# The attention output computed with tokens on partitions, turned back by a DMA transpose from the fifth pair of chunks on, and the order of operations planned anew

## The chip, the cores and the metric

The kernel runs on one core of a Trainium2 chip. The metric is the device time of one execution in microseconds. Three runs of the kernel before gave 177.81 us as the median (177.77 to 180.62). The profile is of one execution, taken by the hardware profiler.

The engines are named as in the profile: PE is TensorE (matmuls; PEld is its weight loads), DVE is VectorE, ACT is ScalarE, POOL is GpSimd and SP is SyncE, which here only issues DMAs. L756 is line 756 of the kernel before; lines of the changed kernel lie 33 to 91 further down.

## The reference

A gated linear attention (4 batches x 8 heads, 768 tokens, head size 48) is followed by a feed-forward layer with a squared ReLU (3,072 tokens, 384 to 2,048 to 384). Inputs and output are float32.

```python
for t in range(S):                       # q, k, v, alpha: (4, 8, 768, 48)
    state = alpha[:, :, t, :, None] * state + np.einsum('bhd,bhe->bhde', k[:, :, t], v[:, :, t])
    y[:, :, t] = np.einsum('bhd,bhde->bhe', q[:, :, t], state)
x = y.transpose(0, 2, 1, 3).reshape(B * S, H * D)        # (3072, 384)
h = x @ w_in                                             # w_in (384, 2048)
r = np.maximum(h, 0.0)
out = (r * r) @ w_out                                    # w_out (2048, 384)
```

## The kernel before

**Tiling.** The 3,072 tokens are 24 chunks of 128, worked as 12 pairs (g = 0 to 11). Three pairs are one batch. In a pair, tokens 2p and 2p+1 lie on partition p, so that a tile holds 256 tokens, and each chunk c of the pair is one half of the partitions. All 8 heads go together.

**Stages of a pair.** Four loads bring alpha, k, q and v (384 KB each as counted by the profile, line 474, SP queue) into one of four RAW buffers. *decay* takes logarithms, sums them over the tokens on PE (L502, L504), takes exponentials on ACT and scales q and k on DVE (qks, L523). *turned* transposes qks, so that features lie on partitions (qkt): on PE in the first three pairs, from the fourth on by a DMA transpose of 16 blocks of 128x128 on the SP queue (L586). *scores* (L634) multiplies q and k in quarters of the array (64x64), and DVE applies the causal mask (pm, L644). *carry* (L663) adds the pair to the state (DVE L681, POOL L683). *mixed* (L702) computes y: 48 matmuls of masked scores with v (pm, vbf) and up to 24 of q with the state before the chunk (qkt, sbf). In the first pair of a batch the first chunk has no state, and 12 of the 24 fall away. v and the state are the stationary operand and 128 columns move, so y comes out with features on partitions, as the next stage needs it. As a head has 48 features and a matmul gives 64 rows, heads are cut into 12 shares. ACT copies y from PSUM to XT (L739).

**Feed-forward layer.** *up*: 8 units of 6 matmuls a pair (L756, 128x256), ACT ReLU (L760), DVE square (L762, gt). *down*: 8 units of 4 matmuls a pair (L780, 128x384), after every fourth an ACT copy (L787) and a store of 192 KB on the SP queue (L789). The last chunk's down is cut in two halves (L800).

**Weights.** w_in and w_out come in four pieces each on the POOL queue (L446, L449), cast to bf16 on the way; the first waits for alpha of pair 1. The loads of pair 2 wait for the second piece of w_out (OPENS).

**What sets the order.** Nothing is ordered by hand. Each stage adds operations with a work in ns and a due time `at`, counted in half pairs: `2 * g + OFF[name]` (EARLY for pairs 0 and 1, MID for pair 2). A list scheduler (`order`) goes through a model of the engines and of the DMA queues and puts, on each engine, the due operation that is ready first in its queue. It fixes the order of instructions on each engine and each DMA queue; on the chip each engine goes through its list in order and waits on semaphores. The model has constants: LATENCY between engines, RESERVE added to every hand-over after the start, LATE added to the landing of loads, rates of transfers (PAIR, ROWS, TURN), SWITCH for the change between full and quartered array on PE. Where PE is planned to be idle before the first down, `fill` puts matmuls on zeros (L769, `busy`), 512 columns each.

Of the kernel before, what the change touches and what calls it, by code (L numbers as in the profile page):

```python
# [15 lines left out]
class Op:  # L16


    def __init__(self, n, eng, fn, work, at, dma=None, nbytes=0, rate=0.0):
# [7 lines left out]
        self.form = None  # L27


class Program:  # L30
# [4 lines left out]
    RESERVE, LATE = 200, 1200.0  # L35
    AHEAD = 4
    BEGIN = {"SP": 1200.0, "POOL": 2200.0}
    LANDING = {"SP": 900.0, "POOL": 1400.0}
    PAIR, ROWS, TURN = 320.0, 390.0, 135.0
    PACKET = {PAIR: 384.0, TURN: 256.0}  # L40
    LONG = 1792.0
    HOLD = 2500.0
    SWITCH, STICK = 95.0, 1.0

# [7 lines left out]
    def add(self, eng, fn, work, at, reads=(), writes=(), dma=None, nbytes=0, rate=0.0, behind=None, form=None,  # L52
            drain=None):
# [25 lines left out]
        op.form = form  # L79
# [3 lines left out]
    def order(self):  # L83
# [26 lines left out]
        def transfer(limit):  # L110

            while now[0] < limit:
# [20 lines left out]
                if queue[first][0][1] <= 1e-3:  # L133
                    op = queue[first].pop(0)[2]
                    op.landed = op.landed0 = end + self.LANDING[first]
                    if op.at > -2 and op.rate == self.PAIR:
                        op.landed += self.LATE
                    if first == "SP":
                        landed.append(op.landed0)
# [10 lines left out]
        form = None  # L150
        while left:
# [38 lines left out]
            if e == "PE":  # L190
                if op.form != form:
                    op.work += self.SWITCH
                form = op.form
            free[e] = t + op.work
# [21 lines left out]
        self.programs = programs  # L216

# [85 lines left out]
def bass_gla_recurrent__then__act_relu_squared_kernel(  # L303
# [31 lines left out]
    NS, NU, NAC, NRO = 5, 3, 3, 2  # L335
    NGT, NRR, NOS = 3, 4, 8
# [17 lines left out]
    XT = sb("xt", [128, KT, G * TW], BF16)  # L354
# [72 lines left out]
    WH = 4  # L427
    FIRST = 2
    TURN = 3
    SELF = 12  # L430


    RUNS = [(1, 3, 8)]
    OPENS = {2: 5}
    pieces = [(w, n) for w in ("in", "out") for n in range(WH)]
    last_weight, last_load = [None], [None]

    def weights(at, run):
        x0 = sum(r[2] for r in RUNS[:run])
        w0, j0, n0 = RUNS[run]  # L440
        for x in range(x0, x0 + n0):
            which, i = pieces[x]
            gate = raw(w0, j0) if x == x0 else []
            if which == "in":
                w = DFF // WH
                fn = lambda g, i=i, w=w: g.dma_start(WIN[:, :, i * w:(i + 1) * w], win_src[:, :, i * w:(i + 1) * w])  # L446
            else:
                w = FT // WH
                fn = lambda g, i=i, w=w: g.dma_start(WOUT[:, i * w:(i + 1) * w, :], wout_src[:, i * w:(i + 1) * w, :])  # L449
            last_weight[0] = add("POOL", fn, 770, at, reads=gate, writes=[("w" + which, i)], dma=f"w{which}{i}",  # L450
                                 nbytes=DM * DFF * 4 // WH, rate=(305.0, 305.0, 370.0, 370.0, 395.0)[min(x, 4)],
# [12 lines left out]
    def loads(g, at):  # L464
        b, t0, r = g // NW, (g % NW) * TW, g % NRAW
        for j, src in ((3, alpha), (0, k), (1, q), (2, v)):
            s = src[b, :, t0:t0 + TW, :].rearrange("h (p i) d -> p h (i d)", i=2)
            dst = RAW[:, r, j, :].rearrange("p (h e) -> p h e", h=H)
            gate = [("w" + pieces[OPENS[g]][0], pieces[OPENS[g]][1])] if g in OPENS and j == 3 else []
            cuts = (0, 1) if g == 0 and j == 3 else (None,)  # L470
            for X in cuts:
# [5 lines left out]
                                   nbytes=TW * HD * 4 // len(cuts), rate=pr.PAIR, behind=last_load[0])  # L477
# [9 lines left out]
    def decay(g, at):  # L487
# [19 lines left out]
        add("PE", sums, 265, at + 0.02, reads=lab + ["hinc"], writes=[key])  # L507
# [388 lines left out]
```

## Time and profile before

| | |
|---|---|
| median of three runs | 177.81 us (177.77 to 180.62) |
| the profiled execution | 177.77 us, its span 175.8 us |
| granted TensorE clock | 1.000 |
| PE / DVE / ACT / POOL busy | 168.7 / 116.5 / 116.2 / 18.6 us |
| up matmuls L756 | 576, 74.3 us busy |
| down matmuls L780 | 368, 71.2 us busy |
| y matmuls L702 | 576 and 240, 10.4 and 8.6 us busy |
| first up unit, last PE matmul starts | 17.1 us, 173.1 us |
| traffic | 31.83 MB, 75,993 packets |

Busy times of PE overlap: a matmul's length in the profile covers its way through the array, and the next one starts before it ends. What a group of matmuls takes is read from start to start in the timeline. Idle time of an engine that is not on the chain that ended last costs nothing. "issue" is time in which the engine waited for nothing that the profile shows.

### The profile page before, as it was taken

How to read it: one execution, taken by the hardware profiler on the slowest of the kernel's cores; microseconds unless marked ns; L12 is line 12 of the kernel's file. 1: busy time of each engine (PE TensorE's matmuls, PEld its weight loads, DVE VectorE, ACT ScalarE, POOL GpSimd, SP SyncE). 2: the span in 40 equal slices, each digit the busy share in tenths (PEclk: the TensorE clock that was granted, in tenths of full speed). 3: DMA queues.
4: the chain of work that ended last, by engine and by line, in shares of the span. 5: the costliest groups of instructions: out<-in, count | busy, mean ns of one | idle time of the engine just before them, and what ended most of it. 6: DMA issues, size and time to landing. Idle time of an engine off the chain costs nothing.

```text
span 175.8 us, 6062 instructions
## 1 busy us (share of the span) xinstructions
PE 168.7 (96%) x2648; PEld 123.7 (70%) x2648; DVE 116.5 (66%) x251; ACT 116.2 (66%) x235; POOL 18.6 (11%) x35
## 2 busy tenths in 40 slices
PE   7889979999999999999999999999999999999994
PEld 2556658775677777777777776777777777767763
DVE  7895925589979597887965966946836733621410
ACT  4774555695885888879788869747546544645631
POOL 4089300001100201001002001001002000000000
PEclk9999999999999999999999999999999999999999
DMA  5999999999999999999999998901901701101112
GB/s 131 303 300 179 197 203 244 278 318 301 239 248 277 250 261 246 307 180 306 243 235 312 258 265 239 141 28 50 164 4 48 164 4 48 45 4 45 45 45 90
DMA packets 75993, 31.83 MB, mean 181 GB/s; under 512 B 69184, under 2 KB 75968, under 8 KB 75968
## 3 DMA queue, kind: packets, MB, share of 16 engines
q1 hardware_dynamic: 72256, 28.32, 65.0%
q0 software_dynamic: 3712, 3.15, 11.6%
q8 instruction: 20, 0.33, 0.7%
q14 instruction: 5, 0.04, 0.1%
HBM read 25.17 MB, written 4.72 MB: 170 GB/s over the span
## 4 chain that ended last, share of the span: by engine, by line
PE 87%; DVE 3%; ACT 3%; DMA 3%; issue 2%; SPq 1%
PE psH L756 35%; PE psO L780 34%; PE psG L702 8%; PE psG L634 4%; DMA raw<-in_q_dram 3%; DVE pm L644 2%; PE psG L663 2%; ACT xt L739 2%; PE psO L800 2%; PE psG L502 1%; DVE qks L555 1%; ACT rr L760 1%; SPq L474 1%; PE psG L574 1%; DVE ust L681 1%
## 5 line engine op out<-in xcount | busy, mean ns | idle before, releaser
L760 ACT ACTIVATE rr<-psH 128x512 bf16<-128x512 f32 x96 | 56.9, 599 | 35.5 <-PE psH L756 34.6
L756 PE MATMUL psH<-xt,win 128*128 128x256 bf16 x576 | 74.3, 273 | 0.5 <-ACT xt L739 0.4
L780 PE MATMUL psO<-wout,gt 128*128 128x384 bf16 x368 | 71.2, 326 | 0.0
L756 PEld LDWEIGHTS psH<-xt,win 128*128 128x128 bf16 x576 | 54.8, 98 | 13.9 <-ACT xt L739 0.8
L762 DVE TENSOR_TENSOR gt<-rr 128x512 bf16<-128x512 bf16 x96 | 39.8, 425 | 36.7 <-ACT rr L760 36.3
L780 PEld LDWEIGHTS psO<-wout,gt 128*128 128x128 bf16 x368 | 34.5, 98 | 17.2
L644 DVE TENSOR_TENSOR pm<-psG,mask 128x512 bf16<-128x512 f32 x48 | 30.9, 684 | 1.2 <-PE psG L634 1.2
L523 DVE TENSOR_TENSOR qks<-raw,asb 128x768 bf16<-128x768 f32 x20 | 18.4, 956 | 8.1 <-ACT asb L512 8.1
L683 POOL TENSOR_TENSOR sbf<-ust,acp 128x192 bf16<-128x192 f32 x16 | 8.8, 551 | 119.1 <-DVE ust L681 119.1
L739 ACT ACTIVATE xt<-psG 128x384 bf16<-128x384 f32 x24 | 12.6, 596 | 6.6 <-PE psG L702 6.6
L787 ACT ACTIVATE osb<-psO 128x384 f32<-128x384 f32 x23 | 11.4, 494 | 5.2 <-PE psO L780 4.8
L702 PEld LDWEIGHTS psG<-pm,vbf 64*64 64x64 bf16 x576 | 8.4, 107 | 3.7 <-issue 1.8
L702 PE MATMUL psG<-pm,vbf 64*64 64x128 bf16 x576 | 10.4, 218 | 0.6 <-DVE qks L555 0.3
L493 DVE TENSOR_TENSOR raw<-raw 128x384 f32<-128x384 f32 x20 | 10.6, 551 | 0.0
L512 ACT ACTIVATE asb<-psG 128x384 bf16<-128x384 f32 x20 | 9.9, 495 | 1.1 <-PE psG L504 0.8
L702 PE MATMUL psG<-qkt,sbf 64*64 64x128 bf16 x240 | 8.6, 220 | 1.0 <-issue 1.0
L634 PEld LDWEIGHTS psG<-qkt 64*64 64x64 bf16 x384 | 5.8, 106 | 4.3 <-issue 2.4
L634 PE MATMUL psG<-qkt 64*64 64x128 bf16 x384 | 8.1, 219 | 0.6 <-ACT qkt L617 0.4
L769 PE MATMUL psO<-warm 128*128 128x512 bf16 x22 | 7.5, 463 | 1.1 <-DVE warm L391 1.1
L485 ACT ACTIVATE vbf<-raw 128x768 bf16<-128x768 f32 x10 | 8.4, 841 | 0.0
L681 DVE TENSOR_TENSOR ust<-psG,sbf 128x192 f32<-128x192 f32 x15 | 5.3, 355 | 2.6 <-POOL sbf L683 1.9
L498 ACT ACTIVATE lab<-raw 128x384 bf16<-128x384 f32 x10 | 5.2, 520 | 2.2 <-DVE raw L493 2.2
(65 smaller groups left out, 99.5 us busy)
## 6 DMA issues: line engine op xcount, KB each, us to landing
raw<-in_k_dram SPq DMA_DIRECT2D x12, 384.0 KB, 5.0
raw<-in_q_dram SPq DMA_DIRECT2D x12, 384.0 KB, 5.6
raw<-in_v_dram SPq DMA_DIRECT2D x12, 384.0 KB, 5.4
out_dram<-osb SPq DMA_DIRECT2D x23, 192.0 KB, 2.0
raw<-in_alpha_dram SPq DMA_DIRECT2D x11, 384.0 KB, 4.5
win<-in_moe_w_in_dram POOLq DMA_DIRECT2D x4, 384.0 KB, 7.9
wout<-in_moe_w_out_dram POOLq DMA_DIRECT2D x4, 384.0 KB, 12.4
raw<-in_alpha_dram SPq DMA_DIRECT2D x2, 192.0 KB, 2.8
```

The lines of the kernel that those rows point to most:

```text
L493: add("DVE", lambda e: e.tensor_tensor(dst, a0, a1, ALU.mult), 470, at_, reads=reads, writes=writes)
L512: add("ACT", lambda act, z=z: act.activation(ASB[a][:, z, 0, :], ps[:, 0:HD], AF.Exp, scale=2.0 * z - 1.0), 372, at + 0.04 + 0.02 * z, rea ...
L523: add("DVE", lambda dve, z=z, decays=decays: dve.tensor_tensor(QKS[x][:, z, :, :, 0:D], both(r, z), decays, ALU.mult), 870, at + 0.05 + 0. ...
L634: last = pe.matmul(banks[i, j // 2][0][64 * c:64 * c + 64, col:col + 128].rearrange("p (a b) -> p a b", a=2), QKT[t][64 * i:64 * i + 64, 0 ...
L644: add("DVE", lambda dve, i=i, X=X, ps=ps: dve.tensor_tensor(PMB[m][:, i, 2 * X:2 * X + 2].rearrange("p j n s -> p j (n s)"), ps[:].rearran ...
L702: last = pe.matmul(o, lhsT, rhs, start=(c, n % 2) not in begun, stop=True, skip_group_check=True)
L739: add("ACT", lambda act, ps=ps, base=base: act.activation(XT[:, :, base:base + C].rearrange("f k (p i) -> f k i p", i=2), ps[:, 0:HD].rear ...
L756: last = pe.matmul(ps[:, f * TW:(f + 1) * TW], WIN[:, kt, fj * 128:(fj + 1) * 128], XT[:, kt, g * TW:(g + 1) * TW], start=(kt == 0), stop= ...
L760: add("ACT", lambda act: act.activation(RR[r][:], ps[:], AF.Relu), 480, at, reads=[key], writes=[key, ("rr", r)])
L762: add("DVE", lambda dve: dve.tensor_tensor(gt[:, 2 * u:2 * u + 2, :], rr, rr, ALU.mult), 340, at, reads=[("rr", r)], writes=[("gt", g % NG ...
L780: last = pe.matmul(ps[:, 0:DM], GT[g % NGT][:, fj, tt * 128:(tt + 1) * 128], WOUT[:, fj, :], start=(fj == 0), stop=(fj == FT - 1))
L787: add("ACT", lambda act: act.activation(OSB[o][:], ps[:, 0:DM], AF.Copy), 372, at, reads=[key], writes=[key, ("osb", o)])
```

## The change

1. From the fifth pair on (`BACK = 4`), `mixed_back` takes the place of `mixed`. The masked scores and q are stationary and v or the state moves: 64 matmuls with 48 columns and up to 32 more, y with tokens on partitions. ACT copies it to a new tile YB, contiguously, and a DMA transpose of 6 blocks on the SP queue writes XT. Tokens are in another order there, so the store of these pairs writes rows of the output two apart.
2. XT becomes a ring of six pairs (`NX`), [chunk, block, token] within a pair; up reads it with a view of two chunks.
3. In `mixed` the matmuls with the state become operations of their own.
4. w_in comes in five pieces of 2, 2, 4, 4 and 4 blocks; the w_out pieces are issued as a second run that waits for v of pair 1. The loads of pair 2 wait for the first piece of w_out.
5. The warming matmuls in gaps have 128 columns instead of 512. The changed kernel's PE list has 95, the first seven of them with 512 columns as before; the kernel before has 22.
6. The scheduler gets other constants, a model of PE's instruction blocks (`take`), and other due times. Up of pairs 3 to 11 is due at +1.092 instead of -1.226 half pairs.

```diff
-    RESERVE, LATE = 200, 1200.0
+    RESERVE, LATE = 0, 400.0
+    LATE_BACK = 1000.0
...
-    PAIR, ROWS, TURN = 320.0, 390.0, 135.0
-    PACKET = {PAIR: 384.0, TURN: 256.0}
+    PAIR, ROWS, TURN, EARLY = 325.0, 390.0, 135.0, 200.0
+    PACKET = {PAIR: 120.0, TURN: 256.0}
...
+    BLOCK, AHEAD_OF_ALL, FETCH, CALM, BUSY_UNTIL = 256, 37, 5200.0, 1800.0, 36000.0
+    FILL, SHARE = 58.0, 0.75
...
+                filling = filling and n not in until
+                if filling and used > self.AHEAD_OF_ALL:
+                    gap = 2 * int(max(0.0, t - free[e]) * self.SHARE / self.FILL)
+                    used, there = self.take(used, gap, free[e], 100.0, there)[:2]
+                used, there, late = self.take(used, op.size + 1, t, op.work, there)
+                op.work += late
...
+    def take(self, used, size, t, work, there):
+        late = 0.0
+        block = used // self.BLOCK
+        for b in range(block + 1, (used + size) // self.BLOCK + 1):
+            at = t + late + work * (b * self.BLOCK - used) / size
+            late += max(0.0, there.get(b, 0.0) - at)
+            there[b + 1] = max(at, there.get(b, 0.0)) + self.FETCH - (self.CALM if at > self.BUSY_UNTIL else 0.0)
+        return used + size, there, late
...
-    XT = sb("xt", [128, KT, G * TW], BF16)
+    XT = sb("xt", [128, 2 * NX, KT, C], BF16)
+    YB = sb("yb", [128, 2, HD], BF16, NY)
...
-    RUNS = [(1, 3, 8)]
+    RUNS = [(1, 3, 5), (1, 2, 4)]
...
+    CUTS = {"in": (0, 2, 4, 8, 12, 16), "out": (0, 4, 8, 12, 16)}
...
+    def mixed_back(g, at):
+        t, m, vb, b_ = g % NQT, g % NPM, g % NV, g % NY
+        banks = [bank() for c in range(2)]
+        chunks = [1] if g % NW == 0 else [0, 1]
+        def before(pe, swap):
+            for j in range(NP):
+                for i in range(2):
+                    c = i ^ swap
+                    for n in range(2):
+                        if c in chunks:
+                            h = 2 * j + i
+                            last = pe.matmul(banks[c][0][64 * n:64 * n + 64, D * h:D * h + D],
+                                             QKT[t][64 * i:64 * i + 64, 1, n, j, 64 * c:64 * c + 64],
+                                             SBF[(2 * g + c) % NS][64 * i:64 * i + 64, D + PAD * j:2 * D + PAD * j],
+                                             start=False, stop=True, skip_group_check=True)
+            return last
+        def mm(pe):
+            for h in range(H):
+                for i in range(2):
+                    for c in range(2):
+                        for n in range(2):
+                            last = pe.matmul(banks[c][0][64 * n:64 * n + 64, D * h:D * h + D],
+                                             PMB[m][64 * c:64 * c + 64, h % 2, h // 2, i, 64 * n:64 * n + 64],
+                                             VBF[vb][64 * c:64 * c + 64, i, h, 0:D],
+                                             start=(h, i) == (0, 0), stop=True, skip_group_check=True)
+            return last
...
+            add("ACT", lambda act, c=c, ps=ps: act.activation(YB[b_][:, c, :], ps[:, 0:HD], AF.Copy), 400, at + 0.02 * c + 0.01,
+                reads=[key], writes=[key, ("yb", b_, c)])
+        dst, src = XT[:, 2 * (g % NX):2 * (g % NX) + 2].rearrange("f c k t -> f (c k) t"), YB[b_][:].rearrange("p c f -> p (c f)")
+        add("SP", lambda sp: sp.dma_start_transpose(dst, src), 600, at + 0.04, reads=[("yb", b_, c) for c in range(2)],
+            writes=[("xt", g % NX, c) for c in range(2)], dma="back", nbytes=128 * 2 * HD * 2, rate=pr.TURN)
+
+    def store(o, n, cols=slice(None)):
+        rows, tile = out[n * C:(n + 1) * C, cols], OSB[o][:, 0:DM if cols == slice(None) else cols.stop - cols.start]
+        if n // 2 >= BACK:
+            rows = rows.rearrange("(p i) d -> i p d", i=2)
+        return rows, tile
...
-    OFF = dict(decay=-5.14, turned=-4.136, scores0=-2.842, scores1=-2.061, carry=-3.412, mixed=-1.443, up=-1.226)
-    EARLY = dict(decay=-6.102, turned=-5.566, scores0=-5.314, scores1=-4.089, carry=-5.284, mixed=-3.871, up=-2.03)
-    MID = dict(decay=-5.605, turned=-4.806, scores0=-3.382, scores1=-3.16, carry=-4.451, mixed=-1.982, up=-1.395)
+    OFF = dict(decay=-4.416, turned=-4.123, scores0=-1.903, scores1=-1.843, carry=-2.618, mixed=-1.2, up=1.092)
+    EARLY = dict(decay=-6.061, turned=-5.402, scores0=-5.065, scores1=-3.942, carry=-5.21, mixed=-3.405, up=-1.781)
+    MID = dict(decay=-4.77, turned=-4.502, scores0=-4.464, scores1=-4.122, carry=-3.472, mixed=-1.224, up=-0.846)
```

## The prediction

> **What bounds the kernel now.** I read the totals, then the chain that ended last, then TensorE (PE) in order of time, then the transfers. From the page: span, busy time by engine, the DMA row of the 40 slices (4.4 us each, tenths), one DMA queue, and the chain's shares.
>
> ```profile
> span 175.8 us, 6062 instructions
> ...
> PE 168.7 (96%) x2648; PEld 123.7 (70%) x2648; DVE 116.5 (66%) x251; ACT 116.2 (66%) x235; POOL 18.6 (11%) x35
> ...
> DMA  5999999999999999999999998901901701101112
> ...
> q8 instruction: 20, 0.33, 0.7%
> ```
>
> PE is busy for 96% of the span and carries 87% of the chain, so a PE microsecond saved after the start counts in full, and so does one in which PE stands. The DMA row says that transfers are no spare resource either: 16 engines are full until about 114 us. The last row is PE's own instruction stream being fetched: 0.33 MB in 20 packets, about 16 KB each. PE's timeline has the one place where that shows (start, length, engine, line, operation, number):
>
> ```profile
> 21.62 0.22 PE L702 MATMUL psG<-qkt,sbf 64*64 64x128 bf16 x2
> 22.85 0.35 PE L702 MATMUL psG<-qkt,sbf 64*64 64x128 bf16 x10 [1.01 <-issue]
> ```
>
> Twelve matmuls of one group, with no wait among them, are cut in two by 1.01 us of "issue". By the packets' start times a 16 KB packet ran from 20.52 to 21.47 us, and PE went on 1.38 us after its end: it had run out of instructions. A steady pair of chunks reads so:
>
> ```profile
> 116.33 0.82 PE L756 MATMUL psH<-xt,win 128*128 128x256 bf16 x6
> 117.08 0.86 PE L702 MATMUL psG<-pm,vbf 64*64 64x128 bf16 x48
> 117.77 0.34 PE L702 MATMUL psG<-qkt,sbf 64*64 64x128 bf16 x12
> 117.94 0.42 PE L663 MATMUL psG<-vbf,qks 64*64 64x48 bf16 x32
> 118.19 0.37 PE L702 MATMUL psG<-qkt,sbf 64*64 64x128 bf16 x12
> ```
>
> From start to start: 48 matmuls with 128 columns take 0.69 us (14.4 ns each), 32 with 48 columns 0.25 us (7.8 ns). An up unit is 0.655 us, a down unit 0.65; the 0.75 us from 116.33 to 117.08 leaves 0.1 for a change between full and quartered array.
>
> **The change, part by part** (against the profiled execution: 177.77 us, span 175.8 and 2.0 around it; median of the runs 177.81).
>
> 1. *The y matmuls.* Pairs 4 to 11 leave 72 matmuls with 128 columns (72 x 14.4 ns = 1.03 us) for 96 with 48 (96 x 7.8 = 0.75): 0.28 us less, six times. In pairs 6 and 9, first of a sequence, one chunk has no state: 60 x 14.4 = 0.86 against 80 x 7.8 = 0.62: 0.24 less, twice. Sum **-2.2 us**, all on the path.
> 2. *Changes of array shape.* In the built order I count 54 after the first up unit, 50 before: 4 x 0.1 = **+0.4**.
> 3. *Waits that go.* The stall of 1.01 us at 21.84 goes, since the same block boundary now falls about 19 us into the run, in the up units of pair 0: **-1.0**. The only other PE wait above 0.3 us after 26 us is the up units of pair 2 for xt (0.39 at 47.01); in the new order a down unit more stands ahead of them: **-0.4**. What is late next is part 4.
> 4. *The instruction stream.* PE has 5,325 records (2,648 loads, 2,648 matmuls, 29 separate waits) for 20 packets, some 266 each, or blocks of 256 with a little there at the start. With 60 + 2.04 per matmul the cut above lies on 768 = 3 x 256, and the last seven packets begin 1.1 to 1.3 us after PE enters a block: entering one sends for the next, and one only. From the fourth to the fourteenth packet, among full DMA queues, the median is 1.4 us. So a block is there 1.4 + 0.97 + 1.38 = 3.75 us after PE enters the one ahead of it (3.5 where DMA is idle; 5.8 at the stall above). If PE uses up 256 instructions faster, it stands. Before, mixed and carry of a pair are 104 matmuls, 212 instructions, and by this count no two boundaries after 26 us are nearer than 4.9 us. After, they are 128 matmuls, 261 instructions in about 1.1 us. Going down the new order with the durations above, these distances are below 5 us: block 8 to 9 3.5 us, 10 to 11 1.55, 12 to 13 3.15, 15 to 16 3.8, 19 to 20 2.9. The shortest has 4 matmuls of an up unit, then mixed and carry of pair 5, and hardly any MoE work in it. Shortfall against 3.75 (3.5 in the last): 0.25 + 2.2 + 0.6 + 0 + 0.6 = **+3.7**. Bounds: +2.9 if every block takes 3.5 us, +8 if every one takes 4.9 (the slowest of the fourth to fourteenth); nothing at all is a rival. I take the median. The 73 more warming matmuls (95, 88 of them with 128 columns, for 22 with 512) bring the first boundaries earlier; there PE waits 0.3 to 0.6 us at a time for DVE and ACT anyway, which hides some 0.6 us.
>    The Trainium skill ("Runtime: NRT & Kernel Launch", section "Instruction fetch mechanics") also has blocks of 16 KiB with 256 instructions, but says that the next page is fetched while the current one runs and that a crossing is mostly hidden. The trace agrees for 19 crossings and disagrees for the one with 1.01 us. By that rule of the Trainium skill part 4 is nought and the time 174.6 us.
> 5. *The transpose back.* Eight more DMA transposes of 6 blocks of 128x128, where the old ones have 16. An old one alone is 2,048 packets of 256 bytes in 3.1 us (123.80 to 126.88), issue to landing 5.4. The new one is not in the trace: by bytes 6/16 x 3.1 = 1.2 us, if the price is per call 3.1. I take 1.2. It lies between mixed and up of a pair, which the new due times set 2.3 half pairs apart (before 0.2), some 14 us; it is hidden there. On SP it waits for ACT's copy, and the next pair's alpha load and a store stand behind it; who waits for those are the products of a pair needed 20 us later. Cost nothing; without cover, see the second rival. ACT's copies become contiguous (596 ns each before; 494 in L787, same size): 0.1 us off 16 times, off the path.
> 6. *Attention runs ahead.* Up of a pair now comes late, so mixed of pair 7 stands after 49 up and 40 down units where it stood after 56 and 47: 14 units, 9.1 us sooner; the last mixed 17 units, 11 us. Loads and transposes must come so much sooner. DMA per pair: loads 5.4 us (three pairs in 28.66 to 46.17, less two stores), transpose 3.1, two stores 1.4, back 1.2: 11.1 us. PE between the scores of pairs 4 and 11 has 77 us, 11.0 a pair. That just fits, with no reserve where there was one of some 25 us. I cost it at nothing: PE's stalls of part 4 give DMA 3 us.
> 7. *The start.* Weights in nine pieces (first two half as large, one more issue on POOL, 0.8 us), the loads of pair 2 gated by the first piece of w_out, not the second (2.5 us sooner). The first up unit waited for no weights: at 17.14 it follows scores of pair 1, which wait for the raw loads' chain, and that stands. PE is busy 7.49 of the 8.90 us up to 26: at most 1.4 us to win, as much to lose if w_out's last piece comes later. Nothing, +-1.4.
> 8. *Stores in token pairs*: packets of 1,536 bytes as before; the end (2.4 us after the last matmul) stays. Reserve and transfer constants only act through the order.
>
> Sum: -2.2 + 0.4 - 1.0 - 0.4 + 3.7 = +0.5, so **178.3 us**, practically no change.
>
> **The rivals.**
> A. *The blocks come in time.* If the sequencer holds more than one block ahead, or my count is off by some 30 instructions where distances are short, part 4 is nought and the sum is -3.2: **174.6 us**; with the 1.4 us of part 7, 173.2. For it: 19 silent crossings. Against it: none of those was nearer than 4.9 us. The section of the Trainium skill named in part 4 ("Instruction fetch mechanics") would have it this way.
> B. *Slower: scores wait for the DMA queue.* If a transpose back costs as much as a large one (3.1 us), DMA needs 13.0 us a pair against 11.0: over the seven pairs 14 us late, less the 3 us that PE stands anyhow and 5 us by which the earlier loads can be drawn ahead: **184 us**. It decides from about 1.6 us per transpose (7 x 0.5 is then more than the 3 us). For it: DMA is at 9 throughout, and the SP instruction itself took 2 to 3.9 us at the old transposes. Against it: their packets take 18 ns each, and bytes set the time.
> C. *The turned y costs what it saves.* If the 48-column matmuls are limited by weight loads so that each takes 10.5 ns, 96 cost 1.01 us and part 1 is nought: 180.5 us. Against it: carry's 32, with the same shape, run at 7.8.
>
> **How the numbers follow.** Forecast (part 4 between 2.5 and 8 us, 177 to 182.6): 0.50. A: 0.28. B: 0.15. C or something in the start: 0.07. About 2% (3.5 us) is what a measurement of this kernel can tell from no change, as its three runs reach from 177.77 to 180.62. Faster by that is below 174.3: half of A, 0.14. Slower is above 181.4: B and the upper end of the forecast, 0.22. Within: 0.64. The range 173.3 to 183.5 leaves out part of B and a little of A.
>
> **What would show it.** Part 1: in the new trace mixed's 64 plus 32 matmuls take 0.75 us. Part 4: "issue" gaps of 0.3 to 2.5 us inside groups without waits, the largest in mixed of pair 5, each about 1.4 us after a 16 KB packet ends; A has none. Part 6 and B: PE idle ahead of the scores, released by the transpose's DMA, growing from pair to pair. Part 7: the first up unit at 17 us and continuous PE from 26. I am wrong if PE's gaps after 26 us are below 1 us in all, or if they stand at the scores.

## The result, and the profile after

The changed kernel takes **204.54 us** (median of 4 runs, 203.41 to 205.78) against 177.79 us of the kernel before in the same session (177.18 to 180.62): a ratio of 1.152 (95% interval 1.143 to 1.161), 27 us slower. The forecast was 178.3 us, in a range of 173.3 to 183.5. Some executions of one kernel are up to 4% slower than its others; the ratios here and below leave these out, the medians and ranges have them in.

From the page of the changed kernel: span and instructions, busy time by engine, then the 40 slices (5.0 us each) of PE, of its clock, of the DMA engines and of what they moved, and the chain's shares.

```profile
span 201.4 us, 6601 instructions
...
PE 175.9 (87%) x2905; PEld 127.9 (63%) x2905; DVE 119.6 (59%) x251; ACT 114.5 (57%) x235; POOL 20.4 (10%) x36
...
PE   7889899999999995999999859948995999999900
...
PEclk9999999999999998799999997996998899999985
DMA  5999999999999689994989698988877002111111
GB/s 147 282 262 183 202 209 288 298 318 219 320 229 274 160 244 226 173 302 87 319 135 148 182 192 74 252 172 99 80 84 107 27 32 63 46 42 39 36 50 39
...
PE 68%; DMA 12%; SPq 6%; issue 4%; ACT 3%; DVE 2%; DVEq 0%
```

Three things stand in it. PE is busy for 175.9 us, 7 more than before, yet the span is 25.6 longer: PE has holes (the 5s and the 4) and nothing to do in the last two slices. The DMA row ends in 1s that never stop: in the last 35 us 36 to 63 GB/s flow without a pause, where the kernel before had 0s between its bursts. And DMA has gone from 3% of the chain to 12%.

PE's last matmul ends at 191.05 us, 10.3 us ahead of the end of the span; before it was 2.4. All that runs there is the stores. These are two stretches of the changed kernel (from:to, length, five engines' busy time, PE clock, share of the 16 DMA engines, GB/s), after PE's last matmul:

```profile
191.40:196.40 5.00, 0.00 (x0) 0.00 (x0) 0.00 (x0) 0.02 (x1) 0.00 (x0) 0.89 0.13 50
196.40:201.40 5.00, 0.00 (x0) 0.00 (x0) 0.00 (x0) 0.00 (x0) 0.00 (x0) 0.50 0.12 39
```

and this a stretch of 0.8 us of the kernel before with a single store in it:

```profile
158.60:159.40 0.80, 0.80 (x7) 0.49 (x5) 0.00 (x0) 0.13 (x1) 0.00 (x0) 1.00 0.68 246
```

A share of 0.13 is two engines of 16, and it stays at 0.13 while a queue of stores is waiting. By the packets' times a store of 192 KB, 128 packets of 1,536 bytes and about 65 ns each in both kernels, has 2 packets in flight on the mean (12.8 before) and takes 3.9 to 5.3 us where one with nothing beside it took 0.67 (158.65 to 159.32). The last six stores of whole chunks ran one after the other from 167.76 to 196.42 us, and the last two halves after them.

Earlier on it is the loads that pay. PE's waits in the changed kernel (engine, line, what it waited for: us, times, longest):

```profile
PE psH L843 <- ACT rr L849: 5.9, 2, 3.6
PE psH L843 <- issue: 2.2, 1, 2.2
PE psO L870 <- issue: 2.1, 1, 2.1
...
PE psG L667 <- issue: 0.8, 1, 0.8
PE psG L696 <- issue: 0.6, 1, 0.6
```

The first is the largest, and the chain that ended last shows what is behind ACT's relu there (start, length, what):

```profile
109.60 2.25 SPq L507
111.89 7.25 DMA raw<-in_v_dram
119.16 0.84 ACT vbf L518
120.00 0.49 ACT rr L849
120.54 1.46 PE psH L843 x6
```

The load of v, issued on the SP queue, needed 7.25 us to land, ACT's cast of v waited for it, and the relu that PE's next up unit needs stood in ACT's queue behind that cast. The other 3.6 us, at 136.81, have the same chain. What is issued while such stores run is late: by its packets' times the transpose back took 4.5 us at 121.64 and 4.3 us at 137.97, against 1.1 us (69.52 to 70.63) with no store in its way.

The "issue" waits are stops for instructions, part 4 of the prediction. PE's timeline around the largest, in pair 5 (start, length, line, operation, count):

```profile
75.79 1.27 PE L843 MATMUL psH<-xt,win 128*128 128x256 bf16 x10
79.29 0.59 PE L843 MATMUL psH<-xt,win 128*128 128x256 bf16 x2 [2.23 <-issue]
...
80.15 1.44 PE L870 MATMUL psO<-wout,gt 128*128 128x384 bf16 x4
81.38 1.87 PE L843 MATMUL psH<-xt,win 128*128 128x256 bf16 x10
```

A down unit of 4 matmuls takes 1.24 us to the next start here, where a warm one takes 0.65: after the stop PE's clock is down (the 8 and the 7 in PEclk), by the trace's clock records to half for 3.41 us.

### The profile page after: what moved, and what is told of

It is laid out like the page before. It is cut to its first block, busy times and chain, and to the rows that moved or that the text cites. A ratio compares the mean times of both kernels' runs of the same rounds, so it can differ in the third digit from the quotient of the medians.

```text
span 201.4 us, 6601 instructions
## 1 busy us (share of the span) xinstructions
PE 175.9 (87%) x2905; PEld 127.9 (63%) x2905; DVE 119.6 (59%) x251; ACT 114.5 (57%) x235; POOL 20.4 (10%) x36
## 3 DMA queue, kind: packets, MB, share of 16 engines
q0 software_dynamic: 4112, 3.15, 10.3%
## 4 chain that ended last, share of the span: by engine, by line
PE 68%; DMA 12%; SPq 6%; issue 4%; ACT 3%; DVE 2%; DVEq 0%
PE psH L843 28%; PE psO L870 26%; DMA raw<-in_v_dram 7%; SPq L507 4%; PE psG L667 3%; DMA raw<-in_alpha_dram 3%; DMA raw<-in_k_dram 2%; PE psG L803 2%; PE psG L735 2%; DVE qks L588 1%; PE psO L890 1%; PE psG L696 1%; SPq L879 1%; ACT rr L849 1%; PE psO L858 1%
## 5 line engine op out<-in xcount | busy, mean ns | idle before, releaser
L843 PE MATMUL psH<-xt,win 128*128 128x256 bf16 x576 | 80.0, 281 | 8.4 <-ACT rr L849 5.9
L870 PE MATMUL psO<-wout,gt 128*128 128x384 bf16 x368 | 75.9, 336 | 2.4 <-issue 2.1
L843 PEld LDWEIGHTS psH<-xt,win 128*128 128x128 bf16 x576 | 56.2, 101 | 25.8 <-ACT rr L849 7.7
L716 POOL TENSOR_TENSOR sbf<-ust,acp 128x192 bf16<-128x192 f32 x16 | 9.8, 615 | 119.9 <-DVE ust L714 119.7
L858 PE MATMUL psO<-warm 128*128 128x128 bf16 (+1 forms) x95 | 10.2, 250 | 1.1 <-DVE warm L420 1.1
L858 PEld LDWEIGHTS psO<-warm 128*128 128x128 bf16 x95 | 6.3, 101 | 3.0 <-issue 1.7
L818 ACT ACTIVATE yb<-psG 128x384 bf16<-128x384 f32 x16 | 7.0, 489 | 1.6 <-PE psG L792 1.6
L541 ACT ACTIVATE ro<-raw 128x384 f32<-128x384 f32 x10 | 5.3, 529 | 3.6 <-DMA raw<-in_alpha_dram 3.6
L526 DVE TENSOR_TENSOR raw<-raw,ro 128x384 f32<-128x384 f32 x10 | 6.0, 597 | 0.7 <-DMA raw<-in_q_dram 0.7
L803 PEld LDWEIGHTS psG<-vbf,pm 64*64 64x64 bf16 x512 | 4.8, 108 | 1.8 <-issue 1.2
## 6 DMA issues: line engine op xcount, KB each, us to landing
wout<-in_moe_w_out_dram POOLq DMA_DIRECT2D x4, 384.0 KB, 11.1
```

The costliest lines, as they stand in the source:

```text
L526: add("DVE", lambda e: e.tensor_tensor(dst, a0, a1, ALU.mult), 470, at_, reads=reads, writes=writes)
L716: add("POOL", lambda e, u=u, to=to, ac=ac: e.tensor_tensor(to, UST[u][:], ac, ALU.mult), 600, at + 0.05 * c, reads=[("ust", u), ("acp", c_ ...
L843: last = pe.matmul(ps[:, f * TW:(f + 1) * TW].rearrange("p (c t) -> p c t", c=2), WIN[:, kt, fj * 128:(fj + 1) * 128], XT[:, 2 * (g % NX): ...
L858: last = pe.matmul(psO[i % NPO][:, 0:128 * wide].rearrange("p (a b) -> p a b", a=wide), WARM[:], bass.AP(tensor=WARM, offset=0, ap=[[128, ...
L870: last = pe.matmul(ps[:, 0:DM], GT[g % NGT][:, fj, tt * 128:(tt + 1) * 128], WOUT[:, fj, :], start=(fj == 0), stop=(fj == FT - 1))
```

## The experiments

Theory S: the store's address pattern, two rows of 64 tokens each, runs on two DMA engines and explains most of the 27 us. Theory I: what else is lost is PE standing for instructions. The rivals were a transfer-bound stage through the transposes back (rival B of the prediction) and the new order of operations. Runs that were made together share their runs of the kernel before: 178.48 us for the first four, 179.43 and 179.44 for the next eight, 179.85 for the last three (g1 to g3).

### The stores

**e1: 128 consecutive rows per store.**

```diff
-        if n // 2 >= BACK:
-            rows = rows.rearrange("(p i) d -> i p d", i=2)
```

> The changed kernel, but every store writes 128 consecutive rows, as before; for pairs 4 to 11 the rows of the output therefore stand in the tile's order of tokens, not in the reference's. Nothing else differs, the order on every engine is the same. Theory S (the store with rows two apart is two rows of 64 and runs on two DMA engines only, 4 to 5 us instead of 0.7, and holds up the loads and transposes behind it on those two): the tail after the last matmul falls from 10.3 us to 2.4, PE's waits of 16.5, 2.7 and 3.9 us for the ReLU behind a late v load go, and the time is 179 to 183 us; what is left over the kernel before is the instruction stalls near PE matmuls 348, 1368 and 2516 (0.5 to 2.3 us each, with a slower clock for some 3 us after the longer ones) and about 1 us at the start. Rival R (the transposes back, on top of a full DMA queue, are what makes the loads late): only the tail shrinks, 193 to 197 us.

Measured: 184.57 us (182.75 to 185.7), ratio 1.027 (1.016 to 1.038), a little more than theory S expected. PE's waits:

```profile
PE psH L841 <- issue: 2.0, 1, 2.0
PE psG L696 <- issue: 1.4, 1, 1.4
...
PE psG L667 <- issue: 0.9, 1, 0.9
```

The waits for ACT's relu are gone, and so is the long end. Only the pattern of the stores differs, so it costs 1.152 - 1.027 = 0.125 of the time before: 22 of the 27 us, give or take 2.5 by the two intervals. What is left after 26 us are stops for instructions, one of them again in pair 5.

**e2: the same rows as two stores of 64 tokens.**

```diff
...
+        parts = [rows[i] for i in range(2)] if n // 2 >= BACK else [rows[0:64], rows[64:128]]
+        sp.dma_start(parts[0], tile[0:64]).then_inc(pr.sems[f"osb{o}"], 16)
+        return sp.dma_start(parts[1], tile[64:128])
...
```

> The changed kernel with each store cut into two DMAs of 64 rows (even and odd tokens for pairs 4 to 11, upper and lower half of the chunk before), so that no access pattern has 2 as its first dimension; 25 more issues on SP, the order otherwise the same. Theory S: each half runs on 16 engines, as e1 plus at most 2 us: 179 to 184 us. Rival S2 (it is the row pitch of two rows in memory that is slow, not the shape): stores stay above 3 us and the time above 195 us. Rival R: 193 to 198 us.

Measured: 186.30 us (185.75 to 187.19), ratio 1.045 (1.037 to 1.052), above the 184 us that theory S allowed. The rows written are exactly those of the changed kernel; the median landing time of a half is 2.4 us. So what takes 3.9 to 5.3 us is the pattern with a 2 in front, not the interleaved rows in memory. A smaller price is left: the two halves of a store took 1.25 us together late in the run (171.04 to 172.29) where the single store took 0.67; whether that is the rows or the halves is open. Among PE's waits are 2.8 us for instructions in pair 5 (2.0 in e1), 1.3 for ACT's relu and 1.2 for DVE's square; e1's stop of 1.4 us is not among them.

**e3: the kernel before, with only the new pattern of its stores.**

```diff
-            add("SP", lambda sp: sp.dma_start(out[n * C:(n + 1) * C, :], OSB[o][:]), 600, at,
+            add("SP", lambda sp: sp.dma_start(out[n * C:(n + 1) * C, :].rearrange("(p i) d -> i p d", i=2) if n >= 8 else out[n * C:(n + 1) * C, :], OSB[o][:]), 600, at,
...
```

The two half stores of the last chunk are changed in the same way.

> The kernel before, with the stores of pairs 4 to 11 written as two rows of 64, as the change does, and nothing else; the rows of those chunks land in another order than the reference's. Theory S: each such store takes 4 to 5 us on two engines, the last ones make the tail about 8 us longer (186 us) and the loads of the last pairs come later, of which the old order hides most: 184 to 192 us. Rival R: the stores cost only their tail or less, 178 to 181 us.

Measured: 196.59 us (196.25 to 200.0), ratio 1.101 (1.093 to 1.110). After its last matmul, with stores alone:

```profile
185.00:188.00 3.00, 0.00 (x0) 0.00 (x0) 0.00 (x0) 0.00 (x0) 0.00 (x0) 0.94 0.13 50
```

and one of PE's waits on the way there:

```profile
PE psG L634 <- ACT acp L518: 3.4, 1, 3.4
```

The pattern alone makes the old kernel 18 us slower, beyond the 184 to 192 us expected, and by the same two ways: a tail at 0.13 of the DMA engines, 10.35 us long instead of 2.42, and late loads, most of which the expectation had taken to be hidden. Theory S holds from both sides.

### The order and the stops

**e4: the new order with the old y for all pairs.**

```diff
-    BACK = 4
+    BACK = 12
```

> The changed kernel with BACK = 12: y is computed in the old way in all pairs, no transpose back, stores of consecutive rows; the scheduler with its new constants and due times, the weights in nine pieces, the ring of six pairs and the instruction-block model stay. Theory S: about 178 to 182 us, since no store is slow; the stalls of the instruction stream are fewer (104 matmuls in mixed and carry instead of 128). Rival R: the same, 178 to 182. Rival O (the new order itself, with attention 11 us ahead of what DMA delivers, makes the loads late): above 190 us.

Measured: 179.62 us (178.92 to 182.95), ratio 1.007 (1.003 to 1.011). The longest wait of PE after 26 us is 0.5 us. The new order by itself costs 1.3 us, and the first up unit begins at 18.61 instead of 17.14 us. The new y, stores apart, then costs 1.027 - 1.007 = 0.02, or 3.4 us, although PE has less to do for it.

**e6: e1 with the small warming matmuls packed, so that all block boundaries move.**

```diff
-        for i in range(n):
+        widths = [wide] * n if wide > 1 else [4] * (n // 4) + [n % 4] * (n % 4 > 0)
+        for i, wide in enumerate(widths):
```

> The kernel of e1 (stores of 128 consecutive rows, so that the rows of pairs 4 to 11 stand in another order in the output) with the 88 warming matmuls of 128 columns packed into as few as have up to 512 columns: the same columns, 61 matmuls and 61 weight loads fewer, so every boundary between two blocks of 256 instructions falls 61 matmuls later in the work; nothing else moves. Theory I (PE runs out of instructions where two boundaries lie less than 3.75 us apart, and afterwards runs at the low clock for some 3 us): by the new places no two boundaries after 26 us are nearer than about 3.5 us, so the gaps of 1.99 us at 76.71 and 1.37 us at 111.78 in e1 go, and with them about 1.5 us of slow matmuls: 184.6 - 2.0 - 1.4 - 1.5 = 179.7 us (179 to 181). Rival W (the gaps belong to the work at these places, a semaphore or a transfer that is late): the same gaps in mixed of pair 5 and near 112 us, 184 to 185 us.

Measured: 183.78 us (182.94 to 188.06), ratio 1.024 (1.017 to 1.031). The time is that of the rival, but the profile is not. PE's waits:

```profile
PE psH L841 <- ACT rr L847: 2.1, 2, 1.4
PE psG L735 <- DVE pm L677: 1.4, 1, 1.4
...
PE psG L792 <- issue: 0.3, 1, 0.3
```

The stops of 2.0 and 1.4 us of e1 are gone: theory I is right on what they are. Set matmul against matmul, e6 gains 3.7 us on e1 around pair 5 (the stop and the slow clock behind it) and 1.5 us at 112, and loses 1.8 us at the start, 0.5 at 77 (a stop of 0.33 us for instructions), 0.7 between 83 and 91, and 2.9 us between 107 and 130. The loss at the start lies at a single DVE multiply that lasted 1.84 us at 14.71 instead of 0.54, beside a cast on POOL (15.29 to 16.12), and at the slow clock behind PE's wait for it (17.26 to 20.67). The later loss is in the chain that ended last:

```profile
122.16 6.41 DMA raw<-in_v_dram
128.62 0.72 issue
129.98 0.83 PE psH L841 x6
```

PE, no longer stopped, arrives at the relu that stands behind the cast of v, and v has not landed. The loads of v start at 97.34, 109.73 and 122.16 us, 12.4 us apart, with the DMA row full.

**f1: e6 with 1 us of loads less in each of the pairs 7 to 11.**

```diff
+                if j == 2 and g >= 7:
+                    hs = slice(0, 1)
```

> The kernel of e6 with less to load: of v of pairs 7 to 11 only one head of eight is loaded (the other heads are those of an older pair, so y of these pairs is another one); instructions, waits and order are those of e6. In e6 PE's stops for instructions were gone, but it waited 1.4 us at 129.98, 0.65 at 117.27 and 0.3 at 107.13 for ACT's relu, which stood in ACT's queue behind the cast of v, which waited for v's load; between 84 and 128 us the loads of v begin 12.4 us apart (97.34, 109.73, 122.16). Theory D (DMA is the bound there: the eight transposes back and attention's 11 us of lead leave 12.4 us of transfers to a pair, and PE needs 11): 1 us less a pair, the three waits go, 2.2 us less than e6: 181.5 (181 to 182.5). Rival Q (a matter of the order in the queues of SP and ACT, not of the bytes): the waits stay, 183.8.

Measured: 179.21 us (177.41 to 182.51), ratio 0.995 (0.991 to 1.000). The two longest waits of PE after its first matmuls:

```profile
PE psG L641 <- DVE pm L679: 1.0, 1, 1.0
PE psG L737 <- DVE pm L679: 0.7, 1, 0.7
```

No wait for ACT's relu is left among those listed, and none for instructions. Against e6 the trace gains 3.1 us between 84 and 130 us (2.2 were expected); another 2.2 us are the start, where the DVE multiply took 1.12 us in this execution and the clock stayed up, so the time is below the 181 to 182.5 us expected. Same instructions, fewer bytes: what holds e6 there is the transfers, not the order in the queues of SP and ACT.

### The rows in their right order

The rows need not come out in two halves at all, if something on the way puts the tokens in order.

**e8: ACT's relu writes them in order.**

```diff
-        add("ACT", lambda act: act.activation(RR[r][:], ps[:], AF.Relu), 480, at, reads=[key], writes=[key, ("rr", r)])
+        hr, hs = RR[r][:], ps[:]
+        if g >= BACK:
+            hr, hs = hr.rearrange("p (x t i) -> p x i t", x=4, i=2), hs.rearrange("p (x i t) -> p x i t", x=4, i=2)
+        add("ACT", lambda act: act.activation(hr, hs, AF.Relu), 480, at, reads=[key], writes=[key, ("rr", r)])
```

> The changed kernel's output in its right order with stores of 128 consecutive rows: the two halves of a chunk's tokens are put in each other's order by ACT's relu of the up units of pairs 4 to 11 (64 of them, 128x512 each), which writes its result with a stride of two elements. Theory: like e1 (184.6 us, 182.8 to 185.7), since ACT has time to spare: the strided copies of the kernel before took 596 ns against 494 for contiguous ones, 0.1 us x 64 off PE's path. Rival: a down unit follows its last up unit so closely that ACT and DVE end late for it, 0.1 us x 8 pairs or, if the strided write costs 0.5 us each and ACT becomes the bound, 8 x 8 x 0.5 = 32 us more.

Measured: 185.05 us (183.58 to 186.87), ratio 1.030 (1.022 to 1.038), as e1. A strided relu takes 0.75 us on ACT instead of 0.60, and none of PE's longer waits is for it: the one for DVE's square, 1.1 us at 51.26, ends before the first strided relu (75.95). So the rows could have been put in order, without the slow store, for nothing that can be measured here.

**e9: PE reads its moving operand in order.**

```diff
+                        hs = hs.rearrange("p (c t i) -> p c t i", c=2, i=2)
+                        xs = xs.rearrange("p c (i t) -> p c t i", i=2)
```

> The same as e8 with the order made elsewhere: the up matmuls of pairs 4 to 11 (768 with 256 columns) read their moving operand with a step of 64 elements between neighbouring columns, ACT's relu is left as it was. No row of the traces has such a read on PE. Theory: PE reads it at its full rate, 184.6 us as in e1, up units stay at 0.655 us. Rival: each step to another place costs as much as a second read, up units take 1.3 us: 64 x 0.65 = 42 us more, 226 us. I expect the first, with little confidence.

Measured: 230.70 us (230.02 to 235.16), ratio 1.286 (1.279 to 1.294). My expectation fell, the rival's 226 was near. PE's timeline of e9:

```profile
123.73 1.62 PE L847 MATMUL psH<-xt,win 128*128 128x256 bf16 x6
125.19 0.81 PE L872 MATMUL psO<-wout,gt 128*128 128x384 bf16 x4
```

An up unit takes 1.46 us to the next start where it took 0.655, for the same 6 x 256 columns: reading columns that lie 64 elements apart costs 2.2 times as much, in 64 units 51 us of PE, of which 46 reach the time (184.57 us in e1).

### Can the gain of y be had?

Seven kernels test whether PE time that is saved reaches the end.

**e10 and g3: the kernel before, its stop of 1.01 us taken away by moving the block boundaries 36 or 15 matmuls.**

```diff
-    def busy(pe, n):
-        for i in range(n):
+    def busy(pe, n, cut=2):
+        for i in range(n * cut):
...
-    add("PE", lambda pe: busy(pe, 7), 2950, ...)
+    add("PE", lambda pe: busy(pe, 7, 4), 2950, ...)
```

In g3 the last line is `busy(pe, 7, 1)`, so the first seven stay whole.

> The kernel before with its warming matmuls cut smaller (7 of 512 columns into 28 of 128, 15 of 512 into 30 of 256: the same columns, 36 matmuls more), so that every boundary of its instruction blocks falls 36 matmuls earlier in the work. Theory I: the boundary that stopped PE for 1.01 us at 21.84 had 4.7 us behind the one ahead of it and needed 5.8 there; now the two are at 13.5 us and at 19 to 20 us, and no later two are nearer than 4.9 us, so the stop goes: 178.5 - 1.0 = 177.5 against the kernel before on the same chip, 0.6% less. Rival W: the stop stays where it was (in mixed of pair 1), the same time.

> The kernel before with only its 15 later warming matmuls of 512 columns cut in two, 15 matmuls more ahead of the work, so that no two block boundaries after 13 us are nearer than about 5 us. Theory I: no stop at 21.84 and none later, 1 us less than the kernel before (0.6%). If a stop of over 1 us stands elsewhere, as in e10, a block needs more than 5 us in some places and the distances can't be made safe by so small a shift: the same time.

Measured: e10 180.19 us (177.97 to 182.17), ratio 0.999 (0.994 to 1.004); g3 180.36 us (178.63 to 183.59), ratio 1.001 (0.996 to 1.006). In neither trace does PE stand in mixed of pair 1, so theory I was right again on the stop. The 1 us (0.6%) is not won: e10's interval just reaches it, g3's leaves it out.

e10 is the weaker test. In its trace PE's full clock begins at 10.11 us instead of 5.91, the work ahead of the stop runs 1.6 us later than in the kernel before, and at 26 us nothing is won. The reason given in g3's expectation does not hold either: what stood at 112 us in e10 was no stop for instructions. PE's timeline of e10, in an execution of 181.79 us:

```profile
112.04 0.42 PE L634 MATMUL psG<-qkt 64*64 64x128 bf16 x16 [1.79 <-ACT acp L518]
112.39 1.38 PE L756 MATMUL psH<-xt,win 128*128 128x256 bf16 x6
```

Behind it its chain has a load of alpha (105.52, 5.37 us).

g3 shows it better. Matmul against matmul its trace is 0.9 us ahead of the kernel before at 26 us, 0.4 behind at 60 and 1.7 behind after 90. One of its waits on the way, at 53 us, is for the transfer of a transpose:

```profile
PE psG L634 <- DMA qkt<-qks: 0.7, 1, 0.7
```

and a wait of 1.1 us stands at the end of this chain:

```profile
83.09 6.46 DMA raw<-in_v_dram
...
89.57 0.02 ACT vbf L485
...
90.32 0.59 ACT rr L760
...
90.95 0.83 PE psH L756 x6
```

So by this trace transfers hold the kernel before too, although PE is busy for 96% of its span: what PE won ahead of the last loads came back as waits for transfers. One execution of each was profiled, so the sizes are rough.

**f2, f3, f4: y turned back from pair 6, 4 or 8 on, rows ordered by the relu, the old due times for the first pairs, the boundaries moved.** For f2:

```diff
-    BACK = 4
+    BACK = 6
...
-    add("PE", lambda pe: busy(pe, 7, 4), 2950, ...)
+    add("PE", lambda pe: busy(pe, 3, 4) and busy(pe, 16), 2950, ...)
...
-    EARLY = dict(decay=-6.061, turned=-5.402, scores0=-5.065, scores1=-3.942, carry=-5.21, mixed=-3.405, up=-1.781)
+    EARLY = dict(decay=-6.102, turned=-5.566, scores0=-5.314, scores1=-4.089, carry=-5.284, mixed=-3.871, up=-2.03)
```

> The changed kernel with y turned back by DMA from the seventh pair of chunks on instead of the fifth, its rows put in order by ACT's relu (as in e8), the due times of the first two pairs as in the kernel before (EARLY), and 16 of the warming matmuls of 512 columns at the start cut to 128 columns so that 12 matmuls more stand ahead of the work. By the rows (up 0.655, down 0.65, 14.2 ns and 7.9 ns a matmul, 0.095 a change of shape) PE's work after the first up unit is 0.9 us shorter than that of the kernel before; no two block boundaries after 26 us are nearer than about 3.7 us, so no stop of 1 us: 178.5 - 0.9 - 1.0 = 176.6 us, 1% faster. Rival D (transfers are the bound): waits of some 2 us take it back, 178.5, the same.

> As f2, but y turned back from the fifth pair on as in the changed kernel, and the 74 small warming matmuls packed two by two (34 fewer) so that by count no two block boundaries after 26 us are nearer than 3.7 us. PE's work is 1.4 us shorter than before: 178.5 - 1.4 - 1.0 = 176.1 if nothing waits; with the waits for DMA that e6 showed (2.2 us) 178.3. I expect the second.

> As f2, but y turned back from the ninth pair on (four transposes back, the first near 90 us, three of them after the loads have ended) and 21 warming matmuls more than in the changed kernel. PE's work is 0.2 us shorter than before, block boundaries at least 3.6 us apart: 178.5 - 0.2 - 1.0 = 177.3, and transfers have the room that e6 lacked. If it is slower than f2 and f3, transfers are not what holds those.

Measured: f2 182.58 us, ratio 1.016 (1.010 to 1.022); f3 184.83 us, ratio 1.029 (1.020 to 1.037); f4 182.76 us, ratio 1.016 (1.008 to 1.024). All three missed. PE's waits of f2:

```profile
PE psH L841 <- ACT rr L850: 1.6, 2, 0.9
PE psH L841 <- DMA win<-in_moe_w_in_dram: 1.6, 3, 1.2
```

With the old due times the first up unit is ready before its weights; f3 and f4 wait for them 1.5 and 1.8 us. Behind that come waits for ACT's relu near 50 us. In f3 PE also stood for instructions, at 70.53 us, although its boundaries had been laid at least 3.7 us apart by count:

```profile
PE psH L841 <- issue: 1.6, 1, 1.6
```

The packet that ended this stop ran from 69.41 to 70.51 us. f4 has the room for transfers late in the run and is no faster than f2, so these runs do not show by themselves what holds them.

**g1, g2: the same from pair 6 or 8 on, with the whole start of the kernel before.**

```diff
...
-    RUNS = [(1, 3, 5), (1, 2, 4)]
+    RUNS = [(1, 3, 8)]
...
-    CUTS = {"in": (0, 2, 4, 8, 12, 16), "out": (0, 4, 8, 12, 16)}
+    CUTS = {"in": (0, 4, 8, 12, 16), "out": (0, 4, 8, 12, 16)}
...
```

> y turned back from the seventh pair on, rows put in order by ACT's relu, and the start of the kernel before: its four pieces of w_in and four of w_out in one run, the second pair's gate on their sixth piece, its due times and transfer constants for the first pairs. Model from rows: PE's work after the first up unit 0.5 us shorter than in the kernel before, its stop of 1.01 us gone, so 178.5 + 0.9 (this chip's 179.4 of the last runs) - 1.5 = 177.9 if up begins at 17.1 us and nothing waits for DMA after it. If the transposes back of pairs 6 to 9, which fall among the last loads, hold up v's cast as in e6, 1 to 2 us more: 179 to 180. If it is slower than that, the due times behind the start are at fault, not y.

> As g1 with y turned back from the ninth pair on (four transposes back, at most one beside loads): PE's work equal to that of the kernel before by the model, its stop of 1.01 us gone: 1 us faster than the kernel before if nothing waits, 178.4 against 179.4. Faster than g1: transfers decide; slower than g1 by 0.5: PE's work decides.

Measured: g1 180.49 us (179.17 to 185.7), ratio 1.010 (1.004 to 1.017); g2 180.65 us (179.58 to 181.7), ratio 1.006 (1.002 to 1.011). Neither gained the 1 to 1.5 us expected, and they do not differ by enough to choose between transfers and PE's work. No stop for instructions above 0.5 us is left in either. In their place stand a wait for w_in at the first up unit (1.3 and 1.5 us) and one of 1.3 and 1.1 us near 50 us, behind a load of v that ran 5.48 us in g1 (43.05 to 48.54). No version here that computes the whole result beats the kernel before. The start stays open: why w_in is late with the old pieces and due times was not settled.

## Why the prediction was wrong

**The step that failed is part 8**: "packets of 1,536 bytes as before; the end (2.4 us after the last matmul) stays". The packets are indeed as before, in size and in time. What I did not look at is over how many engines they go: 2 in place of 16. e1 puts 22 of the 27 us on it, e2 and e8 avoid it with every row in its place, and e3, with 18 us in the old kernel, confirms it; the end grew from 2.4 to 10.3 us. The pattern was in the diff and could be read there: `"(p i) d -> i p d", i=2` makes the outermost dimension 2. The Trainium skill has the rule ("DMA: Bandwidth & Descriptors", section "Why a DMA increments its semaphore by 16 and not by 1"): a transfer goes over the largest number of engines up to 16 that divides the slowest dimension of both patterns. By that rule 2 and 128 give two engines, 64 and 64 give 16, and 128 and 128 give 16; the share of 0.13, e2 and e1 agree.

**The first paragraph** said that a PE microsecond saved after the start counts in full, as PE carries 87% of the chain. That is the second error. g3 took 1 us from PE and won nothing; the chain of a run shows what held that run, not how close behind the next chain stands.

**Part 1** was right in size: in e1 mixed and carry of a pair take 1.17 us from start to start (99.38 to 100.55) where they took 1.41 (117.08 to 118.49), 0.24 us less where 0.28 was foretold. So rival C did not come. By the error above the gain did not reach the end. Part 2 is separated by no run.

**Part 3** was wrong for its larger half. The stop at 21.84 did not go: the boundary lies at the 348th matmul, as the count of part 4 has it, but PE came to it at 21.32 us, at scores and not in the up units at 19, and stood for 0.8 us. As g3 shows, its going would not have helped. Of the 0.39 us of pair 2's up units some 0.2 us stayed.

**Part 4** was right in mechanism, and in place and size for the largest stop: foretold 2.2 us in pair 5, measured 2.23, and the stops end 1.3 to 1.6 us after a packet of 16 KB does, where 1.4 were foretold. Moving the boundaries takes the stops away, in e6 and in g3. That speaks against rival A, by which the blocks come in time. The smaller terms were not right. At the 9th and the 13th block, with 0.25 and 0.6 us foretold, no such stop is in the trace; at the 16th, with nothing foretold, PE stood 0.55 us (1.37 in e1). The 2.09 us at 152.08, where 0.6 were foretold, are another matter: e1, with the same instructions, has no stop there, so this one goes with the slow stores, and its packet (151.72 to 152.91) started some 5 us later against the work than in e1 (137.50). It is luck, then, that the sums, 4.9 us in the changed kernel and 3.4 in e1 after 26 us, lie near the 3.7 foretold. What the sum lacked is the slow clock behind a stop of about 2 us: around pair 5 e6 won 3.7 us by taking away a stop of 2.0, so about 1.7 us go to the clock.

**Part 5** had the price of a transpose back too low where it counts. One with nothing beside it took 1.1 us, foretold as 1.2. But three of e6, in the stretch in which pairs are still loaded, took 1.9 to 2.2 us from first to last packet (92.78 to 95.00, 105.54 to 107.46, 117.65 to 119.74); why is open, as few other packets ran beside them. That is above the 1.6 us from which rival B was to decide, and waits of its kind came without slow stores too (e6), though mostly at the relu behind a late v and not, as it had them, at the scores.

**Part 6** is the term that weighs most once the stores are set right. I had 11.1 us of DMA a pair against 11.0 us of PE, saw that there was no reserve, and wrote nothing for it. In e6 it came to 12.4; of the 1.3 us more, 0.7 to 1.0 are the dearer transpose back of part 5, and f1 shows that 3.1 us hang on it. PE's stops did give DMA their time, as I wrote; taking the stops away gives it back.

**Part 7**: the first up unit began at 18.97 us instead of 17.14, 1.8 us later and outside the 1.4 us allowed; e4, where it began at 18.61, says that the new order costs 1.3 us in all.

The chances had slower at 0.22, from rival B and the upper end of part 4; what made it slower was in neither. The range was built from the terms whose price I doubted; the largest came from one that I had not priced at all.

## What to carry to other kernels

When a change alters the address pattern of a transfer, price it by the number of engines it occupies (a window with nothing else in it: share of the DMA engines, GB/s), not by packets and bytes; here a leading dimension of 2 made each store six to eight times as long, and loads behind it came late too. When the bottleneck engine is at 96% and another resource is full up to the same point, a saving on the first may be worth only the distance to the second: take a small known stop away and see whether the time moves, before counting on more. Instruction blocks can be counted ahead, and a few warming matmuls more or fewer move their boundaries; but the count is no guarantee, as f3 shows.

## What the runs showed of the hardware

- A store of 128 packets of 1,536 bytes takes 0.67 us by itself with the pattern 128x384 and 3.9 to 5.3 us with 2x64x384; in the tail two engines move 50 GB/s.
- A DMA transpose of 6 blocks of 128x128 took 1.1 us by itself, 1.9 to 2.2 us among loads (e6), and 4.3 to 4.5 us beside slow stores (changed kernel, 121.64 and 137.97).
- By the clock records PE ran at half speed for 3.41 us (a down unit 1.24 us instead of 0.65) after each of the four stops of 2.09 to 3.58 us in the changed kernel and after those of 2.82 us in e2, 1.99 in e1 and 1.79 in e10. After one of 2.04 us in e8, 1.78 in f3 and 1.37 in e1 it did not. Of two stops of 1.42 us in e6 the one at the start did it (48 matmuls of mixed in 1.27 us instead of 0.70), the one at 128.56 did not. So the length of a stop does not decide alone. The Trainium skill ("TensorE: Matmul & The Clock Gate", section "What's actually happening") has the slow clock begin after an idle window of about 3.4 us; of the stops named here ahead of a slow clock only the one of 3.58 us was that long.
- PE reads a moving operand with 64 elements between neighbouring columns at less than half its rate: 1.46 us instead of 0.655 for 6 matmuls of 256 columns. ACT's strided write costs it 25% (0.75 us instead of 0.60).
- A stop for instructions ends 1.3 to 1.6 us after a packet of 16 KB does (before 1.38; changed kernel 1.27 to 1.47; e1 1.34 to 1.55; f3 1.60). With boundaries laid about 3.5 us or more apart by count, no stop above 0.5 us was left after 26 us in e6, f1, f2 and g3; with 3.7 us by count f3 still stood 1.58 us. So the 3.75 us worked out from the kernel before are no safe distance.
